# Threshold attention and a gated feed-forward on one core: batch 0 without a split, and two tiles of a head as a unit

## The chip, the cores and the metric

The kernel runs on one core of a Trainium2 chip. The metric is the device time of one execution in microseconds (us). Five engines work from queues of their own: TensorE (PE, with its weight loads shown apart as PEld), VectorE (DVE), ScalarE (ACT), GpSimd (POOL) and SyncE (SP), which here issues every transfer. An engine takes its instructions in their written order; engines wait for one another by semaphores.

## The reference

Eight batches of eight heads, 576 positions, 64 numbers a head, all float32; then a feed-forward over rows of 512.

```python
scores = 0.125 * q @ k.T                                   # per batch and head, 576 x 576
thresh = max(scores, -1) - tau                             # tau = 0.02
scores = where(scores >= thresh, scores, -1e9)
attn = exp(scores - max(scores, -1));  attn /= sum(attn, -1) + 1e-9
x = concat of the heads' attn @ v                          # batch, 576, 512
x_prev = x shifted by one position (zeros in front)
xk = mu_k * x + (1 - mu_k) * x_prev;  xr likewise with mu_r
out = sigmoid(xr @ w_r) * (relu(xk @ w_k) ** 2 @ w_v)      # w_k 512x1024, w_v 1024x512, w_r 512x512
```

## The kernel before, in words

TensorE's fast type is float32r, which keeps fewer bits than float32. Nearly every operand is therefore **split** into an upper part `hi` (a copy by ACT into float32r) and a remainder `lo` (the operand less `hi`, by DVE or POOL), and a product is made as hi x hi + hi x lo + lo x hi. All weights are split at the beginning, 20 pieces of 128 x 512 (`wk`, `wr`, `wv`; lines 338 to 388, with `xT` as scratch).

The attention goes by **jobs**: a pair of heads of one batch. A job has nine **tiles**: for each head four of 128 queries, and one (`T`) in which the last 64 queries of both heads share 128 partitions. Batch 0 is cut in two rounds of four jobs, the first with queries 0 to 255, the second with the rest, so that the feed-forward can begin early; the other batches have four jobs each: 36 jobs and 288 tiles in all.

For a job, `raw` (queries and keys, transposed by the host) and `vraw` are loaded. ACT scales the queries (line 404) and makes `hi` (409), POOL makes `lo` (415), and eight transfers per job copy both into `st` (436), stacked so that 128 rows hold hi and lo of one head: two matmul pairs per tile make all three products. For `T`, POOL writes block-diagonal operands `bd` (480). ACT and POOL split `vraw` into `vs` (457, 465).

For a tile: PE writes scores into `s` (507); DVE takes the maximum (533); ACT the threshold (546) and the exponential into `p` (554); DVE masks and sums (562); after every second tile DVE inverts two sums (572, 573), and POOL scales `p` (589). PE turns `p` in five transposes of 128 columns into `pt` (624), a tile of two PSUM banks in **one** buffer: 64 last keys stand with 64 first ones in a transpose of their own. ACT copies `pt` to `phi` (636), DVE takes the remainder into `plo` and, for the last keys, into the free half of `phi` (645, two instructions). `attend` then makes nine products per head and half of the queries (667), ACT copies one half of the result to `r` (681) and DVE adds it into `xT` (690).

When all heads have 256 positions of a batch, a feed-forward **chunk** follows: mixing by POOL and ACT into `xk` (768 to 799), the products with `w_k` (821), relu and square and split (829 to 844), with `w_r` (863), the sigmoid, with `w_v` (885), the gate on DVE (891) and the store (901). The last 64 positions of four batches make one chunk: 18 chunks in all.

The order within each queue is made beforehand by a small planner (`Plan.order`): each step is added with an engine, a supposed duration, a key and the tiles it reads and writes; the planner places the step that could begin first, with the lower key at equal times, and respects the number of buffers of each tag. PSUM's eight banks: `s` 2 x 2, `pt` 1 x 2, `w` 2 x 1.

Of the kernel before, what the change touches and what calls it, by code (L numbers as in the profile page):

```python
# [8 lines left out]
F32 = mybir.dt.float32  # L9
# [200 lines left out]
def tile_threshold_attention_then_rwkv_ffn(  # L210
# [28 lines left out]
    W = 2 * S  # L239
# [11 lines left out]
    add = plan.add  # L251

# [50 lines left out]
    bds = [fixed(f"bd{j}", [P, 2, P], FR) for j in range(2)]  # L303
    for j in range(2):
        add("DVE", 0.3, lambda j=j: V.memset(bds[j].get().bitcast(F32), 0.0), writes=[bds[j]], key=-99)
# [9 lines left out]
    def weight(j, name, w, c, f, key):  # L315
# [7 lines left out]
        def t():  # L323
# [4 lines left out]
            0.06,  # L328
# [66 lines left out]
    def operands(job, key):  # L395
        b, hp = job["b"], job["hp"]
        raw = sbuf("raw", [P, W])
        hi, lo = sbuf("hi", [P, W], FR), sbuf("lo", [P, W], FR)
        job["hi"], job["lo"] = hi, lo
        add("DMA", 0.06, lambda: SY.dma_start(raw.get(), qk[b, hp]), writes=[raw], key=key - 9, kb=576)  # L400
        add(
            "ACT",
            0.57,
# [3 lines left out]
            key=key - 4,  # L407
        )
        add("ACT", 1.1, lambda: A.activation(hi.get(), raw.get(), AF.Copy), reads=[raw], writes=[hi], key=key - 4)  # L409
        for y in range(2):  # L410
            cs = slice(y * S, (y + 1) * S)
            add(
                "POOL",
                1.41,
                lambda cs=cs: G.tensor_tensor(  # L415
                    lo.get()[:, cs], raw.get()[:, cs], hi.get()[:, cs].bitcast(F32), op=ALU.subtract
                ),
                reads=[raw, hi],
                writes=[(lo, y)],
                key=key - 4,  # L420
            )
# [3 lines left out]
        for h in range(2):  # L425
# [4 lines left out]
            for dst, rows, src, n, r in (  # L430
# [8 lines left out]
                add("DMA", 0.06, fn, reads=[r], writes=[(dst, rows.start)], key=key - 3, kb=n // 4)  # L439
        vraw = sbuf("vraw", [P, 2, 5, D])  # L440
        add(
            "DMA",
            0.06,
            lambda: SY.dma_start(vraw.get(), v[b, hp].rearrange("p (h c d) -> p h c d", h=2, c=5)),
# [5 lines left out]
        for h in range(2):  # L450
# [6 lines left out]
                lambda t=t, h=h, ch=ch: A.activation(t.get()[:, :, ch], vraw.get()[:, h], AF.Copy),  # L457
# [8 lines left out]
                    t.get()[:, :, cl], vraw.get()[:, h], t.get()[:, :, ch].bitcast(F32), op=ALU.subtract  # L466
# [5 lines left out]
        if job["tail"]:  # L472
            bd = job["bd"] = bds[job["ji"] % 2]
            for y, src in enumerate((hi, lo)):
                for h in range(2):
                    sl = slice(h * D, (h + 1) * D)
                    add(
                        "POOL",
                        0.21,
                        lambda bd=bd, y=y, src=src, sl=sl: G.tensor_scalar(  # L480
                            bd.get()[sl, y, sl], src.get()[sl, SM:S].bitcast(F32), 1.0, 0.0, op0=ALU.mult, op1=ALU.add
                        ),
                        reads=[(src, None if y == 0 else 0)],
                        writes=[(bd, (y, h))],
                        key=key + job["tat"] - 2,
                    )


    smalls = {}

    def query_tile(x):
        n, job, t = x["n"], x["job"], x["t"]
        key = float(n)
        s = psum("s", [P, 2, 512], 2)
        if t[0] == "T":
            hi, lo, bd = job["hi"], job["lo"], job["bd"]
            prods = [(bd, 0, None, hi), (bd, 0, None, lo), (bd, 1, None, hi)]
        else:
            h, c = t
            st1, st2 = job["st"][h]  # L500
            prods = [(st1, None, c, st1), (st2, None, c, st1)]
        for j, (l, y, c, r) in enumerate(prods):

            def mm(j=j, l=l, y=y, c=c, r=r):
                lt = l.get()[:, y] if c is None else l.get()[:, c * P : (c + 1) * P]
                for z in range(2):
# [3 lines left out]
                        r.get()[:, KT + z * HS : KT + (z + 1) * HS],  # L510
# [6 lines left out]
        def sv():  # L517
            return s.get()[:, :, 0:HS]

        if n % 2 == 0:
            smalls[n // 2] = sbuf("sm", [P, 4, 2], F32, 4)
        sm = smalls[n // 2]
        o = n % 2

        def col(j):
            return sm.get()[:, j, o : o + 1]
# [3 lines left out]
            0.67,  # L532
            lambda: V.tensor_reduce(col(0), sv(), axis=AX.XY, op=ALU.max, negate=True),  # L533
            reads=[s],
            writes=[(sm, (0, o))],
            key=key,
        )
        p = sbuf("p", [P, S], F32, 3)

        def pv():  # L540
            return p.get().rearrange("p (a b) -> p a b", a=2)

        add(
            "ACT",
            0.186,
            lambda: A.activation(col(1), col(0), AF.Identity, bias=small.get()[:, 1:2], scale=-1.0),
            reads=[(sm, (0, o)), (small, 1)],
            writes=[(sm, (1, o))],
            key=key,
        )  # L550
        add(
            "ACT",
            0.625,
            lambda: A.activation(pv(), sv(), AF.Exp, bias=col(0)),  # L554
            reads=[s, (sm, (0, o))],
            writes=[p],
            key=key,
        )
        add(
            "DVE",  # L560
            0.74,
            lambda: V.scalar_tensor_tensor(  # L562
                pv(), sv(), col(1), pv(), op0=ALU.is_ge, op1=ALU.mult, accum_out=col(2)
            ),
            reads=[s, (sm, (1, o))],
            writes=[p, (sm, (2, o))],
            key=key - 0.5,
        )
        x["p"] = p

        def invert():
            V.tensor_scalar(sm.get()[:, 2], sm.get()[:, 2], 1e-9, None, op0=ALU.add)  # L572
            V.reciprocal(sm.get()[:, 3], sm.get()[:, 2])  # L573

        if o == 1:
            add(
                "DVE",
                0.25,
                invert,
                reads=[(sm, (2, 0)), (sm, (2, 1))],  # L580
                writes=[(sm, (3, 0)), (sm, (3, 1))],
                key=key - 0.5,
            )
            for y in (slots[n - 1], x):
                yo, yp = y["n"] % 2, y["p"]
                add(
                    "POOL",
                    0.715,
                    lambda yo=yo, yp=yp: G.tensor_scalar(  # L589
                        yp.get(), yp.get(), sm.get()[:, 3, yo : yo + 1], 0.0, op0=ALU.mult, op1=ALU.add  # L590
                    ),
                    reads=[(sm, (3, yo))],
                    writes=[yp],
                    key=y["n"] - 1.0,
                )
            turn(slots[n - 1])
            turn(x)

    def group(job, h, g):
        if (h, g) not in job["groups"]:  # L600
            job["groups"][h, g] = (
                sbuf("phi", [P, 5, 320], FR, 2),
# [4 lines left out]
    def dests(x):  # L607
        job, t = x["job"], x["t"]
        if t[0] == "T":
            return [(group(job, h, job["tg"]), 2 * P, slice(h * ST, (h + 1) * ST)) for h in range(2)]  # L610
        h, c = t
        return [(group(job, h, c // 2), (c % 2) * P, slice(0, P))]

    def turn(x):
# [410 lines left out]
```

## Time and profile before

| | |
|---|---|
| time, median of 2 runs | 1253.01 us (1251.95 to 1254.08) |
| profiled execution: its time, its span | 1252.39 us, 1250.6 us |
| busy PE, DVE, ACT, POOL | 1067.8, 922.1, 905.9, 784.8 us |
| matmuls | 6832 |
| mean granted TensorE clock | 0.953 |
| DMA moved | 117.97 MB |

The span is from the first to the last instruction of the profiled execution. A busy PE includes the time in which a matmul fills and drains. L624 is line 624 of the kernel before; a wait is put down to the engine and line that released it last.

### The profile page before, as it was taken

How to read it: one execution, taken by the hardware profiler on the slowest of the kernel's cores; microseconds unless marked ns; L12 is line 12 of the kernel's file. 1: busy time of each engine (PE TensorE's matmuls, PEld its weight loads, DVE VectorE, ACT ScalarE, POOL GpSimd, SP SyncE). 2: the span in 40 equal slices, each digit the busy share in tenths (PEclk: the TensorE clock that was granted, in tenths of full speed). 3: DMA queues.
4: the chain of work that ended last, by engine and by line, in shares of the span. 5: the costliest groups of instructions: out<-in, count | busy, mean ns of one | idle time of the engine just before them, and what ended most of it. 6: DMA issues, size and time to landing. Idle time of an engine off the chain costs nothing.

```text
span 1250.6 us, 20299 instructions
## 1 busy us (share of the span) xinstructions
PE 1067.8 (85%) x6832; PEld 957.0 (77%) x6832; DVE 922.1 (74%) x2086; ACT 905.9 (72%) x1726; POOL 784.8 (63%) x902
## 2 busy tenths in 40 slices
PE   0534688898699989999799999999999989997998
PEld 0424577797587978898688898988888878986987
DVE  2887886898787887788878696878779786879100
ACT  3555667686687877787787878888887778786643
POOL 4899775564476737574685857565665567563741
PEclk9976698899899998999999999999999989999999
DMA  7946473333332423233333333313233333320001
GB/s 216 261 147 156 92 170 99 94 88 104 87 86 71 104 77 76 74 96 104 86 88 93 96 96 76 100 60 92 83 94 97 87 99 82 104 69 18 9 18 26
DMA packets 41926, 117.97 MB, mean 94 GB/s; under 512 B 7008, under 2 KB 7008, under 8 KB 41824
## 3 DMA queue, kind: packets, MB, share of 16 engines
q1 hardware_dynamic: 41824, 116.69, 36.0%
q8 instruction: 55, 0.90, 0.3%
q14 instruction: 47, 0.39, 0.1%
HBM read 43.52 MB, written 9.44 MB: 42 GB/s over the span
## 4 chain that ended last, share of the span: by engine, by line
PE 42%; DVE 21%; ACT 14%; DMA 9%; issue 5%; POOL 5%; SPq 2%; POOLq 0%; ACTq 0%; DVEq 0%
PE w L885 10%; PE w L821 9%; PE pt L624 7%; PE s L507 6%; PE w L667 6%; DVE p L562 5%; DVE plo L645 5%; DMA raw<-in_qk 5%; DVE sm L533 4%; PE w L863 4%; ACT phi L636 3%; DVE sm L572 2%; DVE phi L645 2%; SPq L436 2%; ACT p L554 2%
## 5 line engine op out<-in xcount | busy, mean ns | idle before, releaser
L589 POOL TENSOR_SCALAR p<-p,sm 128x576 f32<-128x576 f32 x288 | 214.1, 754 | 201.7 <-DVE sm L573 177.6
L636 ACT ACTIVATE phi<-pt 128x640 fp32r<-128x640 f32 (+1 forms) x320 | 204.6, 648 | 145.0 <-PE pt L624 140.5
L624 PE MATMUL pt<-ident,p 128*128 128x128 f32 x1440 | 221.2, 287 | 93.7 <-DVE phi L645 46.9
L645 DVE TENSOR_TENSOR plo<-pt,phi 128x512 fp32r<-128x512 f32 (+1 forms) x320 | 202.4, 633 | 108.5 <-ACT phi L636 105.6
L624 PEld LDWEIGHTS pt<-ident,p 128*128 128x128 f32 x1440 | 170.7, 147 | 136.0 <-issue 49.4
L562 DVE SCALAR_TENSOR_TENSOR p<-s,sm,p 128x576 f32<-128x576 f32 x288 | 233.9, 814 | 31.1 <-ACT p L554 25.2
L533 DVE TENSOR_REDUCE sm<-s 128x1 f32<-128x576 f32 x288 | 214.8, 752 | 40.8 <-PE s L507 37.3
L821 PE MATMUL w<-xk,wk 128*128 128x256 f32 x1728 | 241.8, 288 | 0.3 <-DVE sg L891 0.3
L821 PEld LDWEIGHTS w<-xk,wk 128*128 128x128 f32 x1728 | 223.5, 192 | 0.8 <-DVE sg L891 0.5
L885 PE MATMUL w<-wv,k 128*128 128x512 f32 x864 | 213.8, 393 | 0.0
L554 ACT ACTIVATE p<-s,sm 128x576 f32<-128x576 f32 x288 | 211.2, 733 | 3.6 <-PE pt L624 3.1
L667 PE MATMUL w<-phi,vs 128*128 128x320 f32 (+1 forms) x640 | 193.9, 324 | 5.9 <-ACT phi L636 5.9
L507 PE MATMUL s<-st 128*128 128x288 f32 x512 | 127.8, 333 | 70.8 <-issue 28.1
L885 PEld LDWEIGHTS w<-wv,k 128*128 128x128 f32 x864 | 157.4, 188 | 28.2
L667 PE MATMUL w<-plo,vs 128*128 128x320 f32 (+1 forms) x512 | 151.5, 316 | 7.2 <-DVE plo L645 7.0
L507 PEld LDWEIGHTS s<-st 128*128 128x128 f32 x512 | 87.5, 204 | 89.4 <-issue 62.4
L667 PEld LDWEIGHTS w<-phi,vs 128*128 128x128 f32 x640 | 130.0, 203 | 8.0 <-ACT phi L636 7.7
L415 POOL TENSOR_TENSOR lo<-raw,hi 128x576 fp32r<-128x576 f32 x72 | 102.7, 1439 | 47.0 <-ACT hi L409 45.0
L844 POOL TENSOR_TENSOR k<-r,k 128x512 fp32r<-128x512 f32 x72 | 93.0, 1291 | 57.1 <-ACT k L834 56.3
L507 PE MATMUL s<-st,st 128*128 128x288 f32 x512 | 116.5, 311 | 0.0
L667 PEld LDWEIGHTS w<-plo,vs 128*128 128x128 f32 x512 | 104.4, 204 | 10.7 <-DVE plo L645 10.6
L863 PE MATMUL w<-wr,xk 128*128 128x512 f32 x432 | 112.2, 397 | 0.3 <-DVE xT L690 0.3
(69 smaller groups left out, 1554.6 us busy)
## 6 DMA issues: line engine op xcount, KB each, us to landing
raw<-in_qk SPq DMA_DIRECT2D x36, 576.0 KB, 5.7
st<-hi SPq DMA_DIRECT2D x72, 288.0 KB, 3.3
st<-lo SPq DMA_DIRECT2D x72, 288.0 KB, 4.6
vraw<-in_v SPq DMA_DIRECT2D x36, 320.0 KB, 2.9
st<-hi SPq DMA_DIRECT2D x72, 144.0 KB, 3.6
st<-lo SPq DMA_DIRECT2D x72, 144.0 KB, 3.6
out<-sg SPq DMA_DIRECT2D x32, 256.0 KB, 2.0
wk<-in_w_k SPq DMA_DIRECT2D x8, 512.0 KB, 11.6
```

Of the source, the lines that this page charges most:

```text
L507: PE.matmul(s.get()[:, z, 0:HS], lt, r.get()[:, KT + z * HS : KT + (z + 1) * HS], start=(j == 0), stop=(j == len(prods) - 1),)
L533: lambda: V.tensor_reduce(col(0), sv(), axis=AX.XY, op=ALU.max, negate=True),
L554: lambda: A.activation(pv(), sv(), AF.Exp, bias=col(0)),
L562: lambda: V.scalar_tensor_tensor(pv(), sv(), col(1), pv(), op0=ALU.is_ge, op1=ALU.mult, accum_out=col(2)),
L589: lambda yo=yo, yp=yp: G.tensor_scalar(yp.get(), yp.get(), sm.get()[:, 3, yo : yo + 1], 0.0, op0=ALU.mult, op1=ALU.add),
L624: lambda c=c, o=o: PE.transpose(pt.get()[:, c, :], p.get()[:, o : o + P], ident.get()),
L636: lambda hi=hi, cs=cs, sl=sl: A.activation(hi.get()[:, :, cs], pt.get()[:, :, sl], AF.Copy),
L645: V.tensor_tensor(d, pt.get()[0:m, y, sl], hi.get()[0:m, y, cs].bitcast(F32), op=ALU.subtract)
L667: lambda j=j, c=c, m=m: PE.matmul(o.get()[:, 0:n], vs.get()[:, c], m.get()[:, c, 0:n], start=(j == 0), stop=(j == len(prods) - 1)),
L821: PE.matmul(h.get()[:, f], l, r, start=(ct == 0 and i == 0), stop=(ct == NCT - 1 and i == 2))
L863: PE.matmul(z.get(), l, r, start=(ct == 0 and i == 0), stop=(ct == NCT - 1 and i == 2))
L885: PE.matmul(vps.get(), l, r, start=(ft == 0 and i == 0), stop=(ft == NFT - 1 and i == 2))
```

## The change

1. **Batch 0 in float32** (`PLAIN = 8` jobs). Its eight jobs have no split: `raw` is loaded straight into a buffer of `st1`, ACT scales the queries, and PE makes scores from it with float32 operands, one product of 64 rows in two halves of 288 columns. There are no `hi`, `lo`, `st` copies, `bd` and no split of `vraw`; `phi` is float32 and has no remainder; `attend` makes five float32 products in place of nine, and ACT copies the result to `xT` and `xE`.
2. **Pairs.** Two neighbouring tiles of one head and half are a unit (`P`), with one `p` of 2 x 576 columns in two buffers (before: three of 576). A unit's tiles are inverted together; `T` is a unit of its own. The host now gives the last 64 keys both before and after the first 512, and the unit's first tile takes its keys from the second place. So the last keys of both tiles lie side by side in `p`, 128 columns, and are turned by one transpose: nine for a pair, where there were ten. `raw` is 64 columns wider.
3. **`pt` of one bank, two buffers.** The transposes of the first 512 keys of a tile fill one `pt`, the last keys of a pair another. The copies to `phi` and `plo` are cut accordingly.
4. **Order.** A job's units are (0,0), T, (1,0), (0,1), (1,1), by head and half; before, `T` came as the sixth of nine tiles. `bd` and `m` have one buffer where they had two. Keys and supposed durations of the planner change, so its whole order does.

```diff
-    W = 2 * S
+    W = 2 * S + ST
-    bds = [fixed(f"bd{j}", [P, 2, P], FR) for j in range(2)]
+    bd = fixed("bd", [P, 2, P], FR)
@@ operands @@
+        if job["plain"]:
+            raw = job["raw"] = sbuf("st1", [P, W], F32, 3)
+            vraw = job["vraw"] = sbuf("vs", [P, 5, P], F32, 3)
+            add("DMA", DQ, lambda: SY.dma_start(raw.get(), qk[b, hp]), writes=[raw], key=key - PREP - 5, kb=576)
...
+            return
@@ scores @@
+        k0 = KT + (ST if unit["kind"] == "P" and y == 0 else 0)
...
+                    lambda z=z: PE.matmul(
+                        s.get()[:, z, 0:HS],
+                        raw.get()[hr, c * P : (c + 1) * P],
+                        raw.get()[hr, k0 + z * HS : k0 + (z + 1) * HS],
+                        start=True,
+                        stop=True,
+                    ),
@@ softmax @@
-        p = sbuf("p", [P, S], F32, 3)
+        p = unit["p"] = sbuf("p", [P, 2, S], F32, PB)
@@ turn @@
-        pt = psum("pt", [P, 5, P], 1)
-        for c in range(5):
-            o = ST + c * P if c < 4 else 0
+        pt = psum("pt", [P, 4, P], 2)
+        for c, o in enumerate(at):
...
+            pt = transposes(p, (y,), [y * (S + ST) + c * P for c in range(4)], n + y - 1.0)
+            upper(
+                pt,
+                lambda cs=cs: hi.get()[:, 0:4, cs],
+                lambda pt=pt: pt.get(),
...
+            if not plain:
+                lower(
+                    pt,
+                    lambda cs=cs: lo.get()[:, :, cs],
...
+        pt = transposes(p, (0, 1), [SM], n + 0.1)
...
+        upper(
+            pt,
+            lambda: hi.get()[:, 4, 0 : 2 * P].rearrange("p (a b) -> p a b", a=2),
+            lambda pt=pt: pt.get()[:, 0:1].broadcast_to([P, 2, P]),
...
+        for y in range(2):
+            mine, other = slice(y * D, (y + 1) * D), slice((1 - y) * D, (2 - y) * D)
+            cs = slice(y * P, (y + 1) * P)
+            lower(
+                pt,
+                lambda cs=cs, other=other: hi.get()[other, 4, cs],
+                lambda mine=mine, pt=pt: pt.get()[mine, 0],
+                lambda cs=cs, mine=mine: hi.get()[mine, 4, cs],
@@ attend @@
+                    lambda c=c: PE.matmul(
+                        o.get()[:, 0:n],
+                        vraw.get()[0 : D if c == 4 else P, c],
+                        hi.get()[0 : D if c == 4 else P, c, 0:n],
+                        start=(c == 0),
+                        stop=(c == 4),
+                    ),
@@ ffn_chunk @@
-            diff = sbuf("m", [P, 2, CH], F32, 2)
+            diff = sbuf("m", [P, 2, CH], F32, 1)
@@ order of a job @@
-    full = [(0, 0), (0, 1), (1, 0), (1, 1), (0, 2), ("T",), (0, 3), (1, 2), (1, 3)]
+    HALF, PLAIN = 1, 8
+    full = [(0, 0), "T", (1, 0), (0, 1), (1, 1)]
+    halves = [(0, 0), (1, 0)], [(0, 1), "T", (1, 1)]
```

How the order moves is seen at two places. First, PE's queue about a third of the way through the program, where it passes from tile to tile. Each transpose into `pt` that waits names the engines that it waits for. Before:

```order
L507 MATMUL s<-st_4291 128x288 [waits DVE_49]
L507 MATMUL s<-st_4291 128x288
L507 MATMUL s<-st_4291,st_4294 128x288 x2
L624 MATMUL pt<-ident,p 128x128 [waits DVE_49,Activation_49,Pool_49]
L624 MATMUL pt<-ident,p 128x128 x4
L507 MATMUL s<-st_4370 128x288 [waits DVE_49]
L507 MATMUL s<-st_4370 128x288
L507 MATMUL s<-st_4370,st_4374 128x288 x2
L624 MATMUL pt<-ident,p 128x128 [waits DVE_49,Activation_49,Pool_49]
L624 MATMUL pt<-ident,p 128x128 x4
```

After, for one unit:

```order
L670 MATMUL pt<-ident,p 128x128 [waits Pool_49]
L670 MATMUL pt<-ident,p 128x128 x3
L566 MATMUL s<-st_4348 128x288 [waits DVE_49,PE_49]
L566 MATMUL s<-st_4348 128x288
L670 MATMUL pt<-ident,p 128x128 [waits Pool_49]
L670 MATMUL pt<-ident,p 128x128 x3
L566 MATMUL s<-st_4348,st_4353 128x288 x2
L566 MATMUL s<-st_4348 128x288 [waits DVE_49,PE_49]
L566 MATMUL s<-st_4348 128x288
L566 MATMUL s<-st_4348,st_4353 128x288 x2
L1011 MATMUL w<-xk,wk_573 128x256 x3
L670 MATMUL pt<-ident,p 128x128 [waits DVE_49]
```

Before, the first of five transposes waits for DVE (the one `pt` comes free) and for POOL (`p` is scaled). Now the two sets of four wait for POOL alone and stand close together, and DVE is waited for only by the single transpose of the last keys.

Second, the beginning of POOL's queue (`p<-p,sm` is the scaling of a tile, `xT_77` and `wk` the weights). Before:

```order
L415 TENSOR_TENSOR lo<-raw,hi 128x576 x2
L465 TENSOR_TENSOR vs<-vraw,vs 128x5x64 x2
L346 TENSOR_SCALAR xT_77<-xT_77 128x512 x2
L388 TENSOR_TENSOR wk_134<-xT_77,wk_134 128x512
L415 TENSOR_TENSOR lo<-raw,hi 128x576 x2
L388 TENSOR_TENSOR wk_153<-xT_77,wk_153 128x512
L346 TENSOR_SCALAR xT_77<-xT_77 128x512
L589 TENSOR_SCALAR p<-p,sm 128x576 x2
```

After:

```order
L648 TENSOR_SCALAR p<-p,sm 128x576 x4
L348 TENSOR_SCALAR xT_77<-xT_77 128x512
L439 TENSOR_TENSOR lo<-raw,hi 128x576
L648 TENSOR_SCALAR p<-p,sm 128x576
L390 TENSOR_TENSOR wk_235<-xT_77,wk_235 128x512
L648 TENSOR_SCALAR p<-p,sm 128x576
```

Before, ten instructions of splits stand ahead of the first scaling; now four tiles are scaled first. The one `lo` among them belongs to batch 1's first job, which is split early.

More of the change, by code (lines that the diff above doesn't have):

```diff
@@ L569, in query_tile @@
[L569 to L575, printed above, removed]
-            add(
[L577 to L582, printed above, removed]
-            )
[L584 to L597, printed above, removed]
+            0.29,
@@ L601, in group @@
             job["groups"][h, g] = (
[L602 removed]
+                sbuf("phi", [P, 5, 320], F32 if job["plain"] else FR, 2),
                 sbuf("plo", [P, 4, 320], FR, 2),
@@ L913, in tile_threshold_attention_then_rwkv_ffn @@
             for hp in range(NPAIR):
[L914 to L924 removed]
+                order = full if part is None else halves[part]
+                job = dict(ji=len(jobs), b=b, hp=hp, first=n, groups={})
+                job.update(tg=int(part == 1), tail=part != 0, plain=len(jobs) < PLAIN, units=[])
+                for u in order:
+                    if u == "T":
+                        job["tat"] = n - job["first"]
+                        job["units"].append(dict(job=job, kind="T", n=n))
+                        n += 1
+                    else:
+                        job["units"].append(dict(job=job, kind="P", h=u[0], g=u[1], n=n))
+                        n += 2
+                jobs.append(job)
     wlist = [
@@ new lines, in tile_threshold_attention_then_rwkv_ffn @@
+    for job in jobs:
+        if job["ji"] + 1 < len(jobs):
+            operands(jobs[job["ji"] + 1], float(jobs[job["ji"] + 1]["first"]))
+        b, seen = job["b"], set()
+        for unit in job["units"]:
+            softmax(unit)
+            if unit["kind"] == "T":
+                turn_last(unit)
+            else:
+                turn_pair(unit)
+                seen.add((unit["h"], unit["g"]))
+            if unit["kind"] == "T":
+                seen.add("T")
+            for h, g in sorted(x for x in seen if x != "T"):
+                waits = job["tail"] and g == job["tg"] and "T" not in seen
+                if not waits and (h, g, "done") not in job["groups"]:
+                    job["groups"][h, g, "done"] = True
+                    attend(job, h, g, unit["n"] + 1.5)
+        if job["hp"] == NPAIR - 1:
+            key = unit["n"] - 30.0
+            for g in sorted({g for h, g in (x for x in seen if x != "T")}):
+                if g == 1:
+                    edge(b, key + 30)
+                ffn_chunk("main", b, g, key)
+                if g == 1 and b % NTB == NTB - 1:
+                    ffn_chunk("end", b - NTB + 1, 0, key + 0.5)
```

464 lines of the change are left out of this document (293 added, 171 removed).

## The prediction, made before the changed kernel ran

> **What bounds the kernel now.** I read the page first: shares of the engines and the span in 40 slices.
>
> ```profile
> PE 1067.8 (85%) x6832; PEld 957.0 (77%) x6832; DVE 922.1 (74%) x2086; ACT 905.9 (72%) x1726; POOL 784.8 (63%) x902
> PE   0534688898699989999799999999999989997998
> POOL 4899775564476737574685857565665567563741
> PEclk9976698899899998999999999999999989999999
> ```
>
> No engine is full on the mean, but the slices fall into parts. In the first five PE is at 6 tenths or less, at a lowered clock in three of them (7, 6, 6), and POOL is nearly full from the second to the fourth; later PE stands at 9 nearly throughout. So I cut the span at three times, 28, 217 and 1167 us, and asked for the busy time of each engine between them.
>
> ```profile
> 28.00:217.00 189.00, 114.58 (x599) 100.32 (x599) 151.61 (x295) 120.06 (x226) 153.10 (x142) 0.82 0.61 158
> 217.00:1167.00 950.00, 873.13 (x5769) 785.41 (x5768) 759.41 (x1771) 740.40 (x1426) 584.59 (x701) 0.97 0.33 85
> 1167.00:1250.00 83.00, 78.98 (x465) 70.17 (x463) 5.70 (x10) 37.66 (x64) 36.90 (x47) 1.00 0.07 20
> ```
>
> Columns: length, then busy time of PE, PEld, DVE, ACT and POOL, then the granted clock, the DMA share and GB/s. The first cut is just behind the first scores, the second where batch 1's first tile begins its softmax, the third at the last transposes. Call the parts start (not shown), batch 0, middle (batches 1 to 7) and tail. In batch 0 POOL and DVE are busy 81% and 80% of 189 us. In the middle PE is busy 92% and everyone else 80% or less. A PE at 92% need not be the bound, because its fills and drains count as busy. The list of waits tells what the attention queues for:
>
> ```profile
> ACT phi L636 <- PE pt L624: 140.5, 135, 3.8
> DVE plo L645 <- ACT phi L636: 105.6, 118, 5.0
> PE pt L624 <- DVE phi L645: 46.9, 40, 3.8
> ```
>
> These three are one ring: transposes into `pt`, ACT copies `phi` out of it, DVE takes the remainder, and only then may the next tile's transposes write `pt`, which has one buffer. The timeline shows one turn in the middle (two tiles of one pair):
>
> ```profile
> 796.87 0.73 ACT L554 ACTIVATE p<-s,sm 128x576 f32<-128x576 f32 x1
> 800.48 0.72 ACT L554 ACTIVATE p<-s,sm 128x576 f32<-128x576 f32 x1
> ...
> 807.13 0.71 PE L624 MATMUL pt<-ident,p 128*128 128x128 f32 x5
> 808.23 0.70 ACT L636 ACTIVATE phi<-pt 128x640 fp32r<-128x640 f32 x1
> 809.07 0.68 DVE L645 TENSOR_TENSOR plo<-pt,phi 128x512 fp32r<-128x512 f32 x1
> 809.77 0.29 DVE L645 TENSOR_TENSOR phi<-pt,phi 64x128 fp32r<-64x128 f32 x1
> 810.26 0.71 PE L624 MATMUL pt<-ident,p 128*128 128x128 f32 x5
> ```
>
> From 807.13 to 810.26 the buffer is taken for 3.13 us, and the middle does 252 tiles in 950 us, 3.77 us each. So the one buffer is held about 83% of the time by a ring of four steps on three engines, each with its own queue: **this ring bounds the middle**, not PE's work.
>
> ```profile
> 1166.92 0.71 PE L624 MATMUL pt<-ident,p 128*128 128x128 f32 x5
> 1167.38 2.39 PE L821 MATMUL w<-xk,wk 128*128 128x256 f32 x18
> ...
> 1190.14 11.66 PE L821 MATMUL w<-xk,wk 128*128 128x256 f32 x96
> ...
> 1217.98 11.66 PE L821 MATMUL w<-xk,wk 128*128 128x256 f32 x96
> ```
>
> Back to back, a transpose costs 0.092 us (0.46 for five), and a feed-forward chunk 27.84 us. The tail is three such chunks, 83 us.
>
> **The start.** Today the first scores need the raw load, its scaling, the split and eight copies through the DMA queue.
>
> ```profile
> 5.53 1.28 ACT L404 ACT_TABLE_LOAD   x1 [5.53 <-DMA raw<-in_qk]
> 6.82 0.78 ACT L404 ACTIVATE raw<-raw,small 128x576 f32<-128x576 f32 x1
> ...
> 26.89 0.82 PE L507 MATMUL s<-st 128*128 128x288 f32 x2 [26.89 <-DMA st<-lo]
> ```
>
> In float32 they need only the scaled raw tile: 6.82 + 0.78 and a handoff, about 8 us in place of 27. The load is 5.6% wider (1216 columns for 1152), which is within that rounding. Two more raw loads stand ahead of the first weight on SP's queue now; they have 8 us of compute to land behind.
>
> **Batch 0.** The eight jobs without a split drop these groups:
>
> ```profile
> L415 POOL TENSOR_TENSOR lo<-raw,hi 128x576 fp32r<-128x576 f32 x72 | 102.7, 1439 | 47.0 <-ACT hi L409 45.0 <-DMA st<-lo 1.8
> L465 POOL TENSOR_TENSOR vs<-vraw,vs 128x320 fp32r<-128x320 f32 x72 | 64.1, 891 | 64.2 <-ACT vs L457 53.8 <-PE w L821 7.8 <-PE s L507 1.9
> L480 POOL TENSOR_SCALAR bd<-hi 64x64 fp32r<-64x64 f32 x64 | 15.4, 241 | 2.4
> L645 DVE TENSOR_TENSOR plo<-pt,phi 128x512 fp32r<-128x512 f32 (+1 forms) x320 | 202.4, 633 | 108.5 <-ACT phi L636 105.6
> L645 DVE TENSOR_TENSOR phi<-pt,phi 64x128 fp32r<-64x128 f32 (+1 forms) x320 | 86.5, 270 | 4.8
> L690 DVE TENSOR_TENSOR xT<-w,r 64x256 f32<-64x256 f32 x128 | 53.8, 420 | 22.6 <-ACT r L681 20.0
> L409 ACT ACTIVATE hi<-raw 128x1152 fp32r<-128x1152 f32 x36 | 41.7, 1160 | 1.9 <-PE s L507 1.7
> L457 ACT ACTIVATE vs<-vraw 128x320 fp32r<-128x320 f32 x72 | 33.2, 463 | 1.9 <-DMA vraw<-in_v 1.5
> ```
>
> POOL: 16 x 1.439 + 16 x 0.891 + 16 x 0.241 = 41.1 us. DVE: 40 x (0.633 + 0.270) + 16 x 0.420 = 42.8 us, and eight short sums more. ACT: 8 x 1.160 + 16 x 0.463 = 16.7 us less, and some 6 us more for smaller pieces (below). Left are 112 us on POOL, 109 on DVE, 110 on ACT. At the shares they hold today (81%, 80%) POOL asks for 138 us, DVE for 136; ACT at 80% too for 138. The 64 copies of `st` leave SP's queue and the DMA engines, which were 61% busy; I count nothing for that, since POOL and DVE bound this part.
>
> PE gets dearer: the split ran two or nine products at the fast type, now there are one or five in float32. The trace has no such matmul. Its bounds:
>
> ```profile
> 803.05 0.42 PE L507 MATMUL s<-st 128*128 128x288 f32 x2
> ...
> 803.31 0.42 PE L507 MATMUL s<-st,st 128*128 128x288 f32 x2
> ...
> L624 PE MATMUL pt<-ident,p 128*128 128x128 f32 x1440 | 221.2, 287 | 93.7 <-DVE phi L645 46.9 <-POOL p L589 19.9 <-ACT sm L546 6.8
> ```
>
> Below: as cheap as the fast type, 0.13 us for 288 columns (0.26 between the starts of two pairs). Above: the only float32 matmuls of the trace, the transposes, at their whole time of 0.287 us per 128 columns, 0.65 for 288. I take 0.52, three quarters of the way up, since the upper row has the operands' type. Per column that is 1.8 ns. Batch 0 then has 64 score products and 16 of its last queries (288 columns), 40 products of 256 columns and 40 of 320, 41.6 + 41.6 us, 164 transposes, 15.1, and 12 us of the first chunk: 110 us. At the granted clock of this part (0.82) and the busy share that PE holds in the middle (92%): 146 us. At the lower price it is 21 + 27 = 48 us, 64 with clock and share, and at the upper one 104 + 27 = 131, or 174. So PE draws level with POOL, and I give batch 0 147 us: it ends at 8 + 147 = **155** in place of 217 (146 to 182 by the bounds).
>
> The Trainium skill ("FP8 and Floating Point Precision", TensorE Precision Notes) says that true float32 takes four passes through the array. Four times the 0.13 of the fast type would be 0.52, the same sum; no run here shows it, and the rule speaks against the change, as PE's share of batch 0 nearly doubles by it.
>
> **The middle.** For a pair of tiles, ten transposes become nine: a batch has 16 pairs, so 7 x 16 x 0.092 = 10.3 us less on PE. In the changed order 0.44 of a feed-forward chunk stands ahead of batch 0's last transposes, in the present one 0.90, which gives 0.46 x 27.84 = 12.8 back. DVE's remainders of a pair stay two large and two small pieces. ACT pays for smaller pieces:
>
> ```profile
> L829 ACT ACTIVATE r<-w 128x512 f32<-128x512 f32 x72 | 42.8, 595 | 46.1 <-PE w L821 45.2 <-POOL vs L465 0.4
> L636 ACT ACTIVATE phi<-pt 128x640 fp32r<-128x640 f32 x256 | 179.5, 701 | 125.5 <-PE pt L624 124.2
> L681 ACT ACTIVATE r<-w 64x256 f32<-64x256 f32 x64 | 24.2, 379 | 12.9 <-PE w L667 11.5
> ```
>
> A pair was 2 x 0.701 and is 2 x 0.595 + 0.379: 0.17 us more, 16 pairs a batch, 2.7 us; four tiles of last queries add about 1 us. In all 7 x 3.7 = 26 us, and ACT goes from 740 to 766 of 950, level with DVE's 759, which gets a few more small inversions. The split of the raw tile is 64 columns wider, 28 x 1.439 x 64 / 576 = 4.5 us of POOL, and its four copies into `bd` come earlier in a job, as the last queries move to second place; POOL has 365 us free in the middle, which hides both. One buffer in place of two for `m` and `bd` I cost at nothing on the same ground; were it not hidden, each of 18 chunks would wait once for a piece like L829's, 11 us.
>
> The ring goes. Four transposes take 0.71 - 0.092 = 0.62 us, one 0.34, so a pair's three turns are 2 x (0.62 + 0.595 + 0.68) + (0.34 + 0.38 + 2 x 0.29) = 5.1 us, and three sets of the handoffs seen above (0.39 + 0.14 + 0.20) another 2.2: 7.3 us on two buffers, 3.6 us a pair where it was 6.3. What is late next is PE itself: 873 - 10 + 13 = 876 us. At the 97% that it reaches in the best stretch of today,
>
> ```profile
> 748.00:886.00 138.00, 134.19 (x885) 120.53 (x885) 104.84 (x250) 114.55 (x217) 88.27 (x103) 1.00 0.34 89
> ```
>
> that is **903 us** in place of 950. Bounds: 950 if nothing is won; 860 if some of its drains, which count as busy, go as well. One wait is added: a unit's exponentials wait for the transposes of the unit before the last, which free its `p`. Behind them on ACT stand the copies out of `pt` and `w`, for which DVE and PE wait; that is a rival below.
>
> **Sum.** 155 + 903 + 83 = 1141 us of span, and 1252.4 - 1250.6 = 1.8 around it: **1143 us**. The profiled execution stands 0.6 us under the median of 1253.01, so no correction.
>
> **Rivals.**
> - *Only the beginning is won.* Other rings (`s`, `w`, the wait for POOL's scaling of `p`) hold the middle at 950. For: in the list of waits ACT's wait for `pt` is long but not alone. Against: 83% for `pt`. 155 + 950 + 83 + 2 = 1190, with the dear float32 1216.
> - *PE at half clock in batch 0.* Where PE was half idle its clock was low:
> ```profile
> 94.00:125.00 31.00, 15.40 (x63) 13.05 (x64) 24.69 (x45) 17.15 (x33) 29.06 (x27) 0.61 0.65 157
> ```
> If float32 is at its upper price (131 us) and the clock stays at 0.61: 131 / 0.61 / 0.92 = 233, end of batch 0 at 241, total 241 + 903 + 83 + 2 = 1229. Against: a PE with twice the work is idle less. The Trainium skill ("TensorE: Matmul & The Clock Gate", Part 1) says the same of idle windows of about 3.4 us; the row agrees in kind.
> - *Slower: the two buffers of `p`.* Three tiles become two pairs, and a unit of last queries takes a whole one. Above, the pair's first exponential starts at 796.87 and its last transposes end at 810.97: 14.1 us, 3.13 of it the ring. Per pair of heads four such lives and one of a single tile (10.5, from 800.48) on two buffers: (4 x 14.1 + 10.5) / 2 = 33.5 us, 937 us in the middle; without the ring (4 x 11 + 10.5) / 2 = 27.2, no bound. It turns slower by over 2% from a life of 16 us; at 17 the middle is 28 x 39.25 = 1099, total 1339.
>
> **How the numbers follow.** Forecast 0.60 (1088 to 1180); only the beginning 0.18 (1180 to 1216); half clock 0.08 (1229, just within 2%); two buffers of `p` 0.06; better than 1088, 0.08. Range: 1088 to 1216, low from a middle of 860 and a batch 0 at 146. A measurement tells 2% from no change: faster holds the first, second and last, 0.86, same the half clock, 0.08, slower 0.06.
>
> **What would show it.** First scores at about 8 us; batch 0's last softmax near 155 with POOL at 112 us busy; float32 scores near 0.52 us apart; the wait of transposes for DVE's remainder nearly gone; the middle 903 us with PE at 97%, DVE and ACT at 85%. Wrong would be: a middle of 950 with PE waiting for POOL's `p`, or exponentials that wait for transposes.

## The result, and the profile after

The changed kernel takes **1178.59 us** (median; 1178.11 to 1179.06) where the one before takes 1253.01: a ratio of 0.9406, interval 0.9366 to 0.9446, 74 us less. The forecast was 1143 (1088 to 1216) with 0.86 on faster by over 2%: direction and range held, the gain was forecast half as large again as it is. From here on, L-numbers of the kernel after are those of the changed code (scores L544 in batch 0 and L566 later, maximum L599, exponential L615, mask L623, scaling by POOL L648, transposes L670, `phi` L681, remainder L687).

The page of the kernel after, its engines and the same slices as shown of before:

```profile
PE 1084.4 (92%) x6728; PEld 932.4 (79%) x6728; DVE 860.7 (73%) x2013; ACT 906.4 (77%) x1918; POOL 748.7 (64%) x854
PE   6788899997999889997999999999999999998998
POOL 1889865656766476646675766656667676653661
PEclk9789899999999999999999999999999999998999
```

PE works from the first slice on, and the lowered clocks of 6 are gone. Cut at the same events (first scores, batch 1's first softmax, last transposes), the busy time of PE, PEld, DVE, ACT and POOL, then clock, DMA share and GB/s:

```profile
8.00:166.00 158.00, 137.13 (x556) 89.37 (x557) 113.41 (x207) 107.93 (x246) 119.73 (x98) 0.89 0.38 127
166.00:1091.00 925.00, 866.41 (x5695) 771.05 (x5696) 740.85 (x1792) 755.99 (x1603) 588.25 (x701) 0.99 0.37 90
1091.00:1176.00 85.00, 80.73 (x480) 71.76 (x479) 5.85 (x10) 40.38 (x69) 40.04 (x50) 1.00 0.07 19
```

The table gives each profiled execution by these parts, also of the experiments below; "mid + tail" is one column since a change of order moves feed-forward between the two. Each ratio is to executions of the kernel before that were made beside that kernel, so it is not exactly the quotient of two times of this table.

| kernel | first scores | batch 0 | middle | tail | mid + tail | time, median | ratio to before, interval |
|---|---|---|---|---|---|---|---|
| before | 26.9 | 189.9 | 950.8 | 83.0 | 1033.8 | 1253.01 | |
| after | 7.8 | 157.8 | 925.0 | 85.7 | 1010.7 | 1178.59 | 0.9406 (0.9366 to 0.9446) |
| split0 | 18.1 | 197.7 | 923.4 | 85.8 | 1009.2 | 1229.79 | 0.9847 (0.9811 to 0.9883) |
| pt1 | 7.8 | 157.8 | 1054.6 | 87.3 | 1141.9 | 1309.24 | 1.0474 (1.0439 to 1.0508) |
| nopair | 7.8 | 163.3 | 973.9 | 89.1 | 1063.0 | 1235.86 | 0.9875 (0.9853 to 0.9897) |
| noscale | 7.8 | 152.5 | 928.4 | 87.7 | 1016.1 | 1177.92 | 0.9424 (0.9398 to 0.9449) |
| nothr | 7.8 | 157.3 | 910.4 | 114.6 | 1025.0 | 1187.46 | 0.9483 (0.9446 to 0.9520) |
| nolow | 7.9 | 158.0 | 890.6 | 107.4 | 998.0 | 1166.76 | 0.9320 (0.9273 to 0.9368) |
| kexp | 7.8 | 162.6 | 926.8 | 90.6 | 1017.4 | 1189.56 | 0.9475 (0.9457 to 0.9493) |
| dcost | 7.8 | 162.6 | 942.3 | 87.0 | 1029.3 | 1200.62 | 0.9586 (0.9551 to 0.9621) |
| less32 | 7.8 | 165.2 | 925.8 | 85.7 | 1011.5 | 1187.14 | 0.9479 (0.9449 to 0.9509) |
| maskp | 6.5 | 158.5 | 995.5 | 91.5 | 1087.0 | 1254.05 | 1.0003 (0.9987 to 1.0019) |
| maskp2 | 6.5 | 155.7 | 967.2 | 102.2 | 1069.4 | 1236.20 | 0.9846 (0.9824 to 0.9867) |
| bmask | 24.6 | 195.4 | 1002.0 | 83.0 | 1085.0 | 1306.85 | 1.0419 (1.0385 to 1.0453) |

So the 74 us are 19 at the start, 32 in batch 0 and 26 in the middle, less 3 in the tail. The waits of the kernel after that answer to the ring, over the whole span:

```profile
ACT phi L681 <- PE pt L670: 60.8, 79, 3.9
PEld pt L670 <- POOL p L648: 52.5, 69, 4.0
DVE plo L687 <- ACT phi L681: 52.4, 65, 5.8
PE pt L670 <- POOL p L648: 28.5, 39, 3.5
PE pt L670 <- DVE plo L687: 7.3, 14, 1.6
```

The transposes' wait for DVE fell from 46.9 us to 7.3, and ACT's wait for transposes from 140.5 to 60.8. DVE's wait for ACT fell less, from 105.6 to 71.3 (52.4 for `plo`, 18.9 for the last keys in `phi`); batch 0 has no remainders any more. In the middle alone, these are the three waits of PE that were longest there, before (217 to 1167 us):

```profile
PE pt L624 <- DVE phi L645: 31.7, 31, 2.5
PE s L507 <- DVE p L562: 9.8, 19, 2.4
PE pt L624 <- POOL p L589: 7.9, 13, 1.6
```

and after (166 to 1091 us):

```profile
PE s L566 <- DVE p L623: 22.2, 34, 2.2
PE pt L670 <- POOL p L648: 18.6, 33, 1.1
PE pt L670 <- DVE plo L687: 7.3, 14, 1.6
```

The ring's wait shrank by 24 us, and two others grew by 23 together: scores that wait for the mask to free `s`, and transposes that wait for POOL's scaled `p`. PE's idle time in the middle fell from 77 to 59 us, as smaller waits of the transposes fell too; the other 7 us of the 26 are busy time (866 for 873). One pair in the middle, from the timeline:

```profile
701.82 0.66 PE L670 MATMUL pt<-ident,p 128*128 128x128 f32 x4
...
702.61 0.60 PE L670 MATMUL pt<-ident,p 128*128 128x128 f32 x4
...
703.45 1.07 ACT L681 ACTIVATE phi<-pt 128x512 fp32r<-128x512 f32 x2
...
704.05 1.29 DVE L687 TENSOR_TENSOR plo<-pt,phi 128x512 fp32r<-128x512 f32 x2 [0.81 <-ACT phi L681]
...
704.80 0.33 PE L670 MATMUL pt<-ident,p 128*128 128x128 f32 x1 [0.35 <-DVE plo L687]
...
705.16 0.38 ACT L681 ACTIVATE phi<-pt 128x256 fp32r<-128x256 f32 x1 [0.20 <-PE pt L670]
...
705.83 0.59 DVE L687 TENSOR_TENSOR phi<-pt,phi 64x128 fp32r<-64x128 f32 x2
705.94 0.60 PE L670 MATMUL pt<-ident,p 128*128 128x128 f32 x4
```

Both buffers are filled within 1.4 us, ACT and DVE work them off in a row, and only the single transpose of the last keys waits (0.35 us) for a buffer.

### The profile page after: what moved, and what is told of

It is laid out like the page before. It is cut to its first block, busy times and chain, and to the rows that moved or that the text cites. A ratio compares the mean times of both kernels' runs of the same rounds, so it can differ in the third digit from the quotient of the medians.

```text
span 1176.3 us, 20089 instructions
## 1 busy us (share of the span) xinstructions
PE 1084.4 (92%) x6728; PEld 932.4 (79%) x6728; DVE 860.7 (73%) x2013; ACT 906.4 (77%) x1918; POOL 748.7 (64%) x854
## 4 chain that ended last, share of the span: by engine, by line
PE 50%; ACT 16%; DVE 16%; POOL 11%; issue 5%; DMA 2%; SPq 0%; POOLq 0%; DVEq 0%; ACTq 0%
PE w L1011 11%; PE s L566 8%; PE pt L670 8%; PE w L1075 7%; PE w L1053 6%; PE w L860 6%; DVE p L623 5%; POOL p L648 4%; ACT p L615 3%; ACT phi L681 3%; DVE plo L687 3%; DVE sm L599 3%; PE w L823 2%; PE s L544 2%; DVE phi L687 2%
## 5 line engine op out<-in xcount | busy, mean ns | idle before, releaser
L648 POOL TENSOR_SCALAR p<-p,sm 128x576 f32<-128x576 f32 x288 | 216.8, 761 | 222.0 <-DVE sm L634 202.7
L681 ACT ACTIVATE phi<-pt 128x512 fp32r<-128x512 f32 (+6 forms) x528 | 227.4, 458 | 65.2 <-PE pt L670 60.8
L623 DVE SCALAR_TENSOR_TENSOR p<-s,sm,p 128x576 f32<-128x576 f32 x288 | 232.8, 815 | 59.1 <-ACT p L615 53.5
L670 PE MATMUL pt<-ident,p 128*128 128x128 f32 x1312 | 216.7, 281 | 39.0 <-POOL p L648 28.5
L599 DVE TENSOR_REDUCE sm<-s 128x1 f32<-128x576 f32 x288 | 211.7, 751 | 49.9 <-PE s L544 28.9
L670 PEld LDWEIGHTS pt<-ident,p 128*128 128x128 f32 x1312 | 155.6, 142 | 85.3 <-POOL p L648 52.5
L615 ACT ACTIVATE p<-s,sm 128x576 f32<-128x576 f32 x288 | 211.9, 736 | 1.1
L687 DVE TENSOR_TENSOR plo<-pt,phi 128x512 fp32r<-128x512 f32 x280 | 172.4, 632 | 54.7 <-ACT phi L681 52.4
L860 PE MATMUL w<-phi,vs 128*128 128x320 f32 (+1 forms) x560 | 157.0, 303 | 2.0 <-ACT r L1019 1.4
L607 ACT ACTIVATE sm<-sm,small 128x1 f32<-128x1 f32 x288 | 83.9, 291 | 60.9 <-DVE sm L599 59.2
L860 PE MATMUL w<-plo,vs 128*128 128x320 f32 (+1 forms) x448 | 124.7, 300 | 2.9 <-DVE plo L687 2.6
L566 PE MATMUL s<-st 128*128 128x288 f32 x448 | 106.1, 318 | 13.3 <-DVE p L623 12.0
L860 PEld LDWEIGHTS w<-phi,vs 128*128 128x128 f32 x560 | 105.6, 189 | 5.4 <-ACT r L1019 2.0
L566 PE MATMUL s<-st,st 128*128 128x288 f32 x448 | 97.7, 299 | 0.0
L566 PEld LDWEIGHTS s<-st 128*128 128x128 f32 x448 | 71.3, 190 | 32.2 <-DVE p L623 23.3
L439 POOL TENSOR_TENSOR lo<-raw,hi 128x576 fp32r<-128x576 f32 (+1 forms) x56 | 83.6, 1498 | 18.8 <-ACT hi L433 17.3
```

The lines of the kernel that those rows point to most:

```text
L566: PE.matmul(s.get()[:, z, 0:HS], lt, r.get()[:, k0 + z * HS : k0 + (z + 1) * HS], start=(j == 0), stop=(j == len(prods) - 1),)
L599: lambda sv=sv, col=col: V.tensor_reduce(col(0), sv(), axis=AX.XY, op=ALU.max, negate=True),
L615: lambda sv=sv, pv=pv, col=col: A.activation(pv(), sv(), AF.Exp, bias=col(0)),
L623: lambda sv=sv, pv=pv, col=col: V.scalar_tensor_tensor(pv(), sv(), col(1), pv(), op0=ALU.is_ge, op1=ALU.mult, accum_out=col(2)),
L648: lambda y=y: G.tensor_scalar(p.get()[:, y], p.get()[:, y], sm.get()[:, 3, y : y + 1], 0.0, op0=ALU.mult, op1=ALU.add),
L670: lambda c=c, o=o: PE.transpose(pt.get()[:, c, :], p.get().rearrange("p y s -> p (y s)")[:, o : o + P], ident.get()),
```

## Experiments

Each kernel is the one after with the edit shown, unless said otherwise. Two theories stood at first: (A) the gain at the beginning is the float32 of batch 0 and the gain of the middle is the ring of `pt`; (B) the beginning gains from the new ring and units too, and the middle from pairs or from order.

**split0: batch 0 with its split, the rest as after.**

```diff
-    HALF, PLAIN = 1, 8
+    HALF, PLAIN = 1, 0
```

> The changed kernel with batch 0 split like the others (PLAIN = 0); pairs, the two one-bank buffers of pt and the place of the last queries stay. Float32 theory: the whole gain of the beginning (51 us up to the end of batch 0) is the missing split, so batch 0 ends near 210 us, the middle stays near 925 us, total 1220 to 1230. Rival: a good part of those 51 us is the transposition ring, which is freed in batch 0 too; then batch 0 ends near 190 and the total is 1195 to 1205.

It took 1229.79 us, 51 more than the kernel after, and nearly all of it lies in the beginning: batch 0 ends at 215.8 us (before 216.8, after 165.6), while the middle is 923.4 beside 925.0. Its windows of batch 0 and the middle:

```profile
18.00:216.00 198.00, 122.63 (x607) 105.03 (x608) 158.60 (x304) 123.13 (x251) 156.80 (x142) 0.76 0.60 166
216.00:1139.00 923.00, 849.88 (x5617) 756.72 (x5615) 744.15 (x1796) 749.91 (x1591) 586.36 (x700) 0.99 0.36 91
```

POOL and DVE are at 79% and 80% of batch 0 again (before 81% and 80%), and the clock is at 0.76 (before 0.82). So float32 gives the whole gain of the beginning, 51 us; with the split in place, pairs, two `pt` buffers and the new order gain only 1 us there together, and the middle's gain does not depend on float32. Theory A holds for the beginning.

**pt1: one buffer of `pt`.**

```diff
-        pt = psum("pt", [P, 4, P], 2)
+        pt = psum("pt", [P, 4, P], 1)
```

> The changed kernel with one buffer of the one-bank pt in place of two. Ring theory: the second buffer is what the middle gained; the middle goes back to 945 to 960 us, the waits of transposes for DVE's remainder come back, total 1200 to 1220. Rival (the middle is held by PE's own stream, and its 25 us came from fewer transposes and a better clock): the middle stays within 10 us of 925, total below 1190.

It took 1309.24 us, 131 more, nearly all in the middle (1054.6), and more than either theory gave. The waits show why:

```profile
ACT phi L681 <- PE pt L670: 190.1, 225, 3.2
PE pt L670 <- DVE plo L687: 62.4, 73, 2.2
```

The wait of transposes for DVE is back (98 us with the 35.2 behind the remainders of the last keys), and ACT's is three times that of after. The expectation did not count turns: before, a pair passes the ring twice, now three times. Seven batches make 7 x (16 x 3 + 4 x 2) = 392 turns, and 1054.6 / 392 = 2.69 us a turn; from the first transpose to the last remainder the buffer is held 85% of the time (mean over all records of `pt`; before 83%). With one buffer the ring is PE's longest wait again, and the second buffer is worth 130 us to the new units.

**nopair: each tile's last keys in a transpose and a `pt` of their own.**

```diff
-        pt = transposes(p, (0, 1), [SM], n + 0.1)
...
+        for y in range(2):
...
+            pt = transposes(p, (y,), [S if y else SM - D], n + 0.1)
+            upper(
```

> The changed kernel with the last keys of each tile turned by a transpose of its own: ten transposes and two small copies for a pair again, all else as changed. If PE's stream bounds the middle: 7 x 16 x 0.092 = 10 us more, and ACT's 16 more pieces a batch add some: 1188 to 1195. If PE has room: within 4 us of 1178.6.

It took 1235.86 us, 57 more than after where 10 to 17 had been expected. Its middle is 973.9 us: **longer than before's 950.8**, with two buffers in place of one. The window of the middle, and the two groups that grew:

```profile
171.00:1145.00 974.00, 893.96 (x5776) 785.51 (x5776) 744.12 (x1796) 783.22 (x1711) 584.78 (x698) 0.98 0.35 85
L681 ACT ACTIVATE phi<-pt 64x128 fp32r<-64x128 f32 x224 | 60.5, 270 | 59.8 <-PE pt L670 56.4
L670 PE MATMUL pt<-ident,p 128*128 128x128 f32 x1440 | 261.8, 289 | 63.9 <-POOL p L648 31.6 <-DVE plo L687 24.9 <-DVE phi L687 4.5
```

PE is busy 28 us more than after and ACT 27 more; ACT stands 56 us in front of the small copies, and transposes wait 29 us for DVE where after has 7.3. The four middles, by buffers and turns of a pair, are:

| | two turns a pair | three | four |
|---|---|---|---|
| one buffer | 951 (before, two banks) | 1055 (pt1) | |
| two buffers of one bank | | 925 (after) | 974 (nopair) |

With the rest of the change in place but the last keys turned apart, two buffers lose 23 us against before; the common transpose brings 49. (Part of either can be the order, see kexp and dcost.) With pt1, this says that the middle gained from the two buffers and the common transpose together: with either one taken away it is slower than before. The prediction had priced it at 10 us of PE, less 19 of ACT that it held hidden.

**noscale: POOL's scaling of `p` left out.** One of the two waits that took the ring's place was tested by taking its work away.

```diff
-        for y in ys:
-            add("POOL", 0.715, lambda y=y: G.tensor_scalar(p.get()[:, y], ...), ...)
```

> The changed kernel without POOL's scaling of p (the division by the sum is left out; transposes follow the mask). Theory that the chain mask, inversion, scaling, transposes is what the middle waits for now: the middle falls by 25 to 45 us, total 1130 to 1155. Rival (PE's stream is the bound): below 12 us, total 1166 to 1178.

The time did not move: 1177.92 us, with a middle of 928.4. POOL lost 185 us of work there (588.25 to 403.26), and the transposes now wait for the step ahead of it:

```profile
ACT phi L670 <- PE pt L659: 100.4, 118, 2.8
PE pt L659 <- DVE p L623: 64.4, 65, 6.1
```

So neither the scaling nor the inversion ahead of it sets the pace of the middle; with them gone, the transposes wait for the mask, and the wait for POOL had only named the last member of that chain. What comes up to the mask is not tested by this.

**maskp, maskp2 and bmask: `s` freed earlier.** Two `s` buffers make a second ring, which the prediction had only in a half sentence: scores, maximum, threshold, exponential, mask, then the next scores. Averaged over all records, a tile holds `s` for 6.93 us before and 6.82 after; 252 tiles on two buffers are 252 x 6.82 / 2 = 859 of 925 us, 93% (before 92%). Such a share alone proves nothing: in pt1, where transposes wait for the one `pt`, `s` is held 7.4 us a tile in the middle, 89%. To free `s` after the exponential, maskp masks `p` itself against exp(-tau); maskp2 also drops the threshold, which is then unused; bmask is the kernel before with maskp's edit.

```diff
-                    pv(), sv(), col(1), pv(), op0=ALU.is_ge, op1=ALU.mult, accum_out=col(2)
+                    pv(), pv(), small.get()[:, 3:4], pv(), op0=ALU.is_ge, op1=ALU.mult, accum_out=col(2)
...
-                reads=[s, (sm, (1, y))],
+                reads=[(small, 3)],
```

> The changed kernel, but the mask compares the exponentials in p with exp(-tau) in place of the scores in s with the threshold, so the scores' buffer comes free after the exponential and not after the mask; the threshold is still computed, unused, so that ACT's load is the same. Theory that the two buffers of s are the ring that holds the middle (held 6.8 us a tile, 92% of the time): they are held 1.1 us less, and the middle falls by 35 to 65 us, total 1115 to 1145. Rival (PE's stream or DVE's load is the bound): the middle stays within 10 us of 925, total 1168 to 1182.

> As maskp, and the unused threshold (288 ACT instructions of 0.29 us) is left out too. If ACT's queue, which stands between the maximum and the exponential, sets how long s is held: a further 10 to 30 us below maskp. If maskp has already reached PE's own stream: within 6 us of maskp.

> The kernel before with the mask of maskp (compares p, frees s after the exponential, threshold still computed). If the one buffer of pt bound the middle of the kernel before, as the prediction said: at most 12 us below 1252. If the ring of s bound it already: 30 us or more below.

They took 1254.05, 1236.20 and 1306.85 us, so maskp is 75 us slower than after. The edit had a price of its own. The mask in the kernel after, then in maskp, as minimum, median and maximum of 288:

```profile
L623 DVE SCALAR_TENSOR_TENSOR p<-s,sm,p x288: 797/818/820, 12.7 to 1081.2; 128x576 f32<-128x576 f32 x144
```

```profile
L631 DVE SCALAR_TENSOR_TENSOR p<-p,small x288: 797/820/2378, 11.5 to 1152.8; 128x576 f32<-128x576 f32 x144
L656 POOL TENSOR_SCALAR p<-p,sm x288: 735/747/2098, 16.0 to 1158.0; 128x576 f32<-128x576 f32 x144
```

and the means, in maskp:

```profile
L631 DVE SCALAR_TENSOR_TENSOR p<-p,small 128x576 f32<-128x576 f32 x288 | 285.5, 1001 | 61.5 <-ACT p L623 58.4
L656 POOL TENSOR_SCALAR p<-p,sm 128x576 f32<-128x576 f32 x288 | 246.2, 864 | 225.9 <-DVE sm L642 193.9 <-PE pt L678 12.5 <-PE w L868 7.3
```

The median stayed, the maximum went from 820 to 2378 ns, and the mean from 815 to 1001; POOL's scaling went from a mean of 761 to 864. Nor was `s` held for less: from the first score to the end of the exponential, which frees it in maskp, it is 7.2 us a tile in the middle, where the kernel after holds it 6.8 up to the end of the mask. So the three runs say nothing on `s`: whether its ring bounds the middle stays open.

**nothr and nolow: ACT's and DVE's load.** nothr leaves out the threshold and compares with the negated maximum in its place; nolow leaves out the remainders of a pair's last keys.

```diff
-                lambda col=col: A.activation(col(1), col(0), AF.Identity, bias=small.get()[:, 1:2], scale=-1.0),
...
-                    pv(), sv(), col(1), pv(), op0=ALU.is_ge, op1=ALU.mult, accum_out=col(2)
+                    pv(), sv(), col(0), pv(), op0=ALU.is_ge, op1=ALU.mult, accum_out=col(2)
```

```diff
-        for y in range(2):
-            ...
-            lower(pt, ..., 0.316, key)
```

> The changed kernel without the threshold on ACT (288 instructions of 0.29 us); the mask compares the scores with the negated maximum instead, so DVE's instruction, its operands and the time at which s comes free stay as they are. If the ring of s, with ACT's queue between maximum and exponential, holds the middle: s is held some 0.3 to 0.8 us less of 6.8, and the middle of 925 us falls by 35 to 80. If PE's stream is the bound: it falls by less than 12, as PE loses nothing.

> The changed kernel without DVE's remainder of the last keys in pairs (two instructions of 0.29 us a pair are left out; 65 us of DVE's 741 in the middle). If DVE's load holds the middle: 40 to 65 us less. If the ring of s and ACT's queue do: 5 to 25 us. If PE's stream does: below 10.

Middle and tail of nothr:

```profile
166.00:1075.00 909.00, 842.01 (x5513) 747.75 (x5512) 742.08 (x1787) 693.05 (x1323) 573.70 (x688) 0.98 0.37 91
1075.00:1189.00 114.00, 109.90 (x659) 98.03 (x657) 7.65 (x13) 54.86 (x95) 55.51 (x62) 1.00 0.06 19
```

and of nolow:

```profile
166.00:1056.00 890.00, 837.97 (x5579) 750.83 (x5578) 672.24 (x1569) 741.07 (x1583) 577.45 (x691) 0.99 0.38 93
1056.00:1163.00 107.00, 102.62 (x598) 90.73 (x596) 6.57 (x10) 50.17 (x86) 51.55 (x59) 1.00 0.07 21
```

Both shorten the middle and lengthen the tail: feed-forward products that stood in the middle (5513 and 5579 records for 5695) come after the last transposes. In sum nothr takes 9 us longer with 55 us less on ACT (851.8 busy in all for 906.4), and nolow 12 us less with 69 us less on DVE in the middle. So ACT's load is not the bound, and DVE's would have given 40 to 65 us by the expectation. The 12 us lie in the range expected of the `s` ring and ACT's queue, but they are no more than a new order alone can do (next two runs).

**kexp and dcost: the order alone.** The planner gets another key for threshold and exponential, or durations of mask and inversion nearer to the measured ones.

```diff
-    KMAX, KEXP, KMASK = 0.0, 0.0, 0.5
+    KMAX, KEXP, KMASK = 0.0, 6.0, 0.5
```

```diff
-                0.74,
+                0.86,
...
-            0.29,
+            0.4,
```

> The changed kernel with the planner's key of threshold and exponential lowered by 6, so that ACT takes them before other work that is ready. Ring of s: the 2.2 us between maximum and exponential shrink, total 1150 to 1170. Rival: the copies out of pt and w then wait in their place and nothing is won, 1172 to 1195.

> The changed kernel with two supposed durations of the planner set to what the trace shows start to start: mask 0.86 us in place of 0.74, inversion 0.40 in place of 0.29; nothing else. If the middle loses its time to an order made for wrong durations: 10 to 35 us less, total 1143 to 1168, and the better version. If the order is not what costs: within 6 us of 1178.6.

Both are slower than after, by 11 and 22 us, with the same instructions. The truer durations did worse. So these two changes of order cost 11 and 22 us, as much as the single removals above moved.

**less32: in batch 0, two of the five products of `attend` in place of five**, to see whether PE's float32 work bounds that part.

```diff
-            for c in range(5):
+            for c in (0, 4):
```

> The changed kernel with two of five float32 products of attend in batch 0 (three are left out; some 20 us of PE's 137 there). If PE bounds batch 0: it ends 18 to 24 us earlier than 166, total 1155 to 1162. If POOL and DVE bound it, as the prediction's sum had nearly level: 0 to 8 us earlier, total 1170 to 1180.

Batch 0 became longer, 165.2 us for 157.8, and the time rose to 1187.14. Its window:

```profile
8.00:173.00 165.00, 148.45 (x520) 91.39 (x521) 108.68 (x207) 113.29 (x255) 120.87 (x99) 0.93 0.36 120
```

Fewer products did not shorten it, but PE was not relieved either: it is busy 148 us there for 137. The order changed with the edit and brought 49 products with `w_r` and `w_v` into the part, 13 us, and the same score products were busy 62 us for 49. So the run does not show whether PE's float32 work bounds batch 0. In kexp and dcost the order alone made the part 5 us longer; noscale, with 24 us less on POOL, shortened it by 5. What bounds batch 0 now stays open.

Of the kernels that leave nothing out none is faster than the changed one.

## Why the prediction was right or wrong

**Start: right.** First scores at 7.82 us, forecast 8:

```profile
6.99 0.78 ACT L415 ACTIVATE st<-st,small 128x576 f32<-128x576 f32 x1
...
7.82 1.81 PE L544 MATMUL s<-st 64*128 64x288 f32 x3 [7.82 <-ACT st L415]
```

**The price of float32: right where products stand back to back.** The profile shows one product as two records (128 for the 64 score products of batch 0). Eight records, four products, at a granted clock of 1.00:

```profile
102.33 2.10 PE L544 MATMUL s<-st 64*128 64x288 f32 x8
```

2.10 / 4 = 0.52 us, the value taken, drain of the last one included. From the four passes that the Trainium skill states ("FP8 and Floating Point Precision", TensorE Precision Notes) and the 0.13 us of the fast type comes an estimate of the same 0.52; the trace agrees with that number, though it shows two records and no passes. Half clock did not come: 0.89 was granted.

**Batch 0: right mechanism, a term mis-sized.** POOL, DVE and ACT had nearly the work summed (120 us for 112, 113 for 109, 108 for 110). PE's work was summed too low and its clock taken too low, and the two made up for each other: 137 us at 0.89 are 122 at full clock for 110, and 110 / 0.82 was 134. The furthest term was the transposes, 29 us busy in batch 0 for the 15 that the back-to-back price gave; scores came to 54 and `attend` to 48 for 41.6 each (these sums overlap a little). The step that failed is "the busy share that PE holds in the middle (92%)": PE came to 137 / 158 = 87%, and the part to 158 us for 147; POOL, DVE and ACT are at 76, 72 and 68%. The forecast set the part by its fullest engine at a share borrowed from another stage, and no engine reached the share. This is 11 of the 35 us by which the forecast was too low.

**Middle: half right, and the largest miss.** That the ring relaxes was right: the wait for DVE is nearly gone, and `pt`'s two buffers are held 56% of the time (mean over all records). The failed step is "What is late next is PE itself ... At the 97% that it reaches in the best stretch of today": PE got 866 / 925 = 94%, and the middle is 22 us longer than forecast. Its busy time was nearly right, 866 us for 876 forecast, so the miss is all idle time, 59 us for 27. Late next are the tiles' softmaxes: PE waits 22.2 us for masks to free `s` and 18.6 for scaled `p`, where it had waited 9.8 and 7.9 before. Two more things were not seen:

- A ring that is far from full still costs. The prediction summed a pair's three turns to 7.3 us, and the records give nearly that, 7.8; but it halved them and then dropped the ring. With four turns (nopair) the buffers are held only 62% of the time, transposes wait 29 us for DVE, and the middle loses against before.
- Idle time of PE cost twice in these runs, since the clock was lower where it idled more. The middle of pt1 has the same number of matmuls as that of after and is busy 43 us longer, at a granted clock of 0.94 for 0.99 (866 x 0.99 / 0.94 = 912):

```profile
166.00:1220.00 1054.00, 909.20 (x5695) 810.82 (x5694) 737.41 (x1791) 763.97 (x1601) 588.36 (x701) 0.94 0.32 79
```

  A share of busy time in one good stretch, at a clock of 1.00, is no limit that another order must reach.

What holds the middle at 925 us is not settled. Taking away POOL's scaling, ACT's threshold and part of DVE's remainders, one at a time, moved middle and tail together by +5, +14 and -13 us, no more than a new order alone does (+7, +19). The `s` ring, with PE's longest wait behind it, is the candidate that was not tested cleanly; a third buffer of `s` needs two banks, which PSUM does not have beside `pt` and `w`, and was not tried.

**Tail.** 85.7 us for 83: a little more feed-forward is left behind the last transposes (480 matmul records for 465). In the forecast's range, the low end is added up as 146 + 860 + 85 = 1091 and not 1088; nothing hangs on it.

**Rivals.** *Only the beginning is won* would have been 1190 with a middle of 950; the middle did gain, but 26 of 47 us, so the truth lies between it and the forecast. Two of the three other rings that this rival named, `s` and the wait for POOL's scaling, are the ones that PE's waits moved to. *Two buffers of `p`* show no wait: ACT is idle before the exponentials for 1.1 us in all.

```profile
L615 ACT ACTIVATE p<-s,sm 128x576 f32<-128x576 f32 x288 | 211.9, 736 | 1.1
```

## What to carry to other kernels

Count the turns a unit of work makes through a ring, not only its buffers: each turn pays its handoffs. Here two one-bank buffers at four turns a pair were 23 us slower in the middle than one two-bank buffer at two, and a common transpose for two tiles' last keys, which saves the fourth turn, was worth 49. Before taking a ring out of a forecast, look at what else the same engine waits for: here the ring's wait gave up 24 us, and the next two in line took 23. When an engine's share is used to forecast a stage, take it from a stage with the same neighbours: here the fullest engine of batch 0 stayed at 87% where the middle's had 92 and the best stretch 97. Where a planner writes the order, measure how far the order alone moves the time (here 11 and 22 us) before an experiment that moves it less is read as a cause.

## What the runs showed of the hardware

A DVE instruction whose two tensors both lie in SBUF can be held up by POOL, and POOL by it. In maskp the mask reads `p` twice, where after reads `s` from PSUM and `p`: most still take 820 ns, some up to 2378, and the mean rises by 23%, while POOL's scaling rises by 14%. The kernel before with the same edit shows it as well, a mean of 1053 ns for 814:

```profile
L570 DVE SCALAR_TENSOR_TENSOR p<-p,small 128x576 f32<-128x576 f32 x288 | 303.0, 1053 | 33.8 <-ACT p L562 26.5 <-POOL lo L423 1.3
```

The trace shows what the long ones wait for. In maskp 104 of the 288 masks take over 900 ns (none in the kernel after), and 99 of these end 603 to 620 ns after a POOL instruction ends, whichever instruction that is. The longest sits behind two of POOL's that follow each other without a gap:

```profile
182.10 1.26 POOL L997 TENSOR_TENSOR xk<-mk,xk 128x512 fp32r<-128x512 f32 x1
182.85 2.38 DVE L631 SCALAR_TENSOR_TENSOR p<-p,small 128x576 f32<-128x576 f32 x1 [0.56 <-ACT p L623]
183.33 1.28 POOL L1042 TENSOR_TENSOR k<-r,k 128x512 fp32r<-128x512 f32 x1
```

It ends at 185.23, 0.62 us after the second (184.61). The other way round, 65 of POOL's 288 scalings take over 800 ns (8 in the kernel after), and 49 of these end 0.53 to 0.62 us after a mask ends.

The Trainium skill ("SBUF — State Buffer", SBUF: two separate sides) calls this an exclusive lock: a DVE operation with two inputs in SBUF and a GpSimd operation that reads SBUF shut each other out for a whole instruction. The fixed distance from the end of the one to the end of the other agrees with that.
